# Reordered early loads and first chunks, a state update without products of zeros, and 64x64 tail products behind q, in an RWKV-7 and GCU kernel

## Chip, cores and metric

The kernel runs on one core of one Trainium2 chip. The metric is the device time of one execution in microseconds, from the runs of the program on that core; a comparison takes the medians of several runs of both kernels on the same chip. The profile is of one further execution.

## What is computed

Inputs r, k, v, w, a, b of shape (4, 8, 768, 40) (batch, heads, steps, head dimension) drive a recurrence with one 40x40 state per batch and head; its outputs, regrouped to 3072 tokens of 320 numbers, go through two matrix products with x * cos(x) between them.

```python
for t in range(768):
    y[:, :, t] = einsum('bhd,bhde->bhe', r_t, state)
    Sa = einsum('bhde,bhe->bhd', state, a_t)
    state = state * w_t[:, :, None, :] - einsum('bhd,bhe->bhde', Sa, b_t) + einsum('bhd,bhe->bhde', v_t, k_t)
x = y.transpose(0, 2, 1, 3).reshape(3072, 320)
h = x @ w_in                 # 320 x 2048
out = (h * cos(h)) @ w_out   # 2048 x 320
```

The two weight matrices come as 8-byte floats.

## The kernel before

**Chunks.** The 768 steps are cut into 24 chunks of C = 32. Within a chunk the recurrence is written as small matrix products, and the 32x32 triangular system that links its steps is solved for all 32 pairs of batch and head: VectorE (DVE) inverts it column by column (`inv_step`), or, for the first two groups of four chunks, in two halves of 16 (`pair_step` on DVE, then `pair_first` and `pair_second` as products on TensorE, PE). Inversion is done for four chunks at a time.

**Preparation of a pair of chunks** is `p1(c)`, four steps: `p1_w` transposes w (and for c < 4 scans it), `p1_a` transposes a and scales it (`a_W`), `p1_b` transposes the scaled b (`bn_b`), `p1_n` makes the products that the inversion starts from (`nps`, copied to `nt` and `noff`), and, before the change, also allocates and fills the tile `inv` on GpSimd (POOL).

**Preparation of one chunk** is `p2(c)`: `p2_v` transposes `vp` and `rp`, `p2_k` transposes `kn`, `p2_g` makes the Gram products (`gram`), from which DVE and ScalarE (ACT) make `ag` and part of `vvm`. `p2_in(c)` copies the landed v and r into `vp` and `rp` on POOL; `p2_kn(c)` makes `kn` and copies v into `vvm`, on POOL. When both have run for a chunk, `landed(c)` puts the loads of k, v and r of chunk c + 1 in the list of later work.

**The chunk itself** is `main(c)`, five steps: `ch_t` (t) transposes the state `qz`, `ch_q` (q) multiplies r with it, `ch_x` (x) and `ch_s` (s) solve, and `ch_z` (z) makes the new state and the outputs: on PE it first writes eight bf16 products of zeros over the whole of two PSUM tiles `dps` (64 rows x 288 columns each), so that all 128 rows, those between 40 and 64 of each half among them, hold defined numbers; then 32 fp32 products of `kn_b` with `vvm` and 32 of `bn_b` with `sm` add to them, each 40 columns of weights on 72 columns. DVE adds the result to `qz` and makes `yt`, POOL scales both. `tokens` (two steps later) writes `yt` to DRAM and, one step after that, reads it back as `xT`, the token-major operand.

**The second part** comes in pieces per pair of chunks g and per group j of 512 inner columns: `first_a` and `first_b` make `ph` = `xT` x `w_in` (two fp32 products of 128 rows per 128 columns, and one of the remaining 64 rows: the tails, `w_in_tail`), ACT and DVE make the cosine and the product `gT`, `second` makes `po`. In `first_b` the tails come ahead of the second half of the full products if the step just before was one of small tiles (`G["small"]`), and behind it otherwise. A tail is K = 64 rows on one half of the array: the two halves hold the two column groups e.

**PE tiles.** Operand positions set the tile: q works in 64x64 tiles (40x40 used), z in 32x64 tiles (32x40 used), the tails in 64x128, the full products in 128x128. Each fp32 product leaves two matmul records in the trace.

**Order.** Everything is one hand-written order (`tc.manual_schedule`), and each engine runs its part of it in that order. `step(work, of_inv, of_w, small)` issues one step, then the work in the list `waiting` that is due (`later(n, work)`: after n further steps), then `of_inv` steps of the inversion and `of_w` steps of the weight conversion. Conversion takes 20 blocks of 512 columns from 8-byte to 4-byte floats in four stages: `fetch` (DMA into `words`), `taken`, `mantissa`, `product` (DVE, ACT, POOL). Lines 964 to 1007 write out the beginning, up to z of chunk 0; `segs` (lines 1032 to 1075) gives, chunk by chunk, the order of the steps, with M as a place for a piece of the second part. `busy(n)` and `kept_busy(n)` put in bf16 matmuls of zeros as fillers.

**Loads.** `load(c, names)` issues four DMAs of 40 KB per name, by default on SyncE's queue (SP), which issues in order; those of a chunk's w, a, b go into buffers by the parity of c. `load(4, "ab")`, `load(5, "a")` and the fetches of the first two blocks of weights stand in the beginning before anything of chunk 1; loads of 6 and 7 come after the first preparation of 4 (`both_a`, lines 874 to 882).

Of the kernel before, what the change touches and what calls it, by code (L numbers as in the profile page):

```python
# [20 lines left out]
def kernel(  # L21
# [322 lines left out]
    def step(work, of_inv=0, of_w=0, small=False):  # L344


        before = list(waiting)
        work()
        G["small"] = small
        for w in before:  # L350
            w[0] -= 1
            if w[0] == 0:
                waiting.remove(w)
                w[1]()
        for steps, n in ((inv_steps, of_inv), (w_steps, of_w)):
            for _ in range(min(n, len(steps))):
                steps.pop(0)()
# [76 lines left out]
    def p1_n(c):  # L434
        ps = at("nps")
        for i in range(2):
            for j in range(4):
                for bb in range(B):
                    for e in range(2):
                        mm(  # L440
                            ps[blk[bb ^ e], e, (4 * i + j) * C : (4 * i + j + 1) * C],
                            G["bT", c + i][half[e], j, blk[bb]], G["aT", c + i][half[e], j, blk[bb]],
                            i == 0 and j == 0,
                        )

        if c % 4 == 0:
            G["nt"] = sb1.tile([P, C, 4, 2, HH], F32, tag="nt", name="nt")
            if c < 8:
                G["noff"] = sb2.tile([P, 4, 2, HH, C], F32, tag="rt", name="noff")
        for e in range(2):  # L450
            nc.scalar.copy(
                G["nt"][:, :, c % 4 : c % 4 + 2, e, :].rearrange("p t c j -> p c j t"),
                ps[:, e, : 2 * HH * C].rearrange("p (c j t) -> p c j t", c=2, j=HH),
            )
        if c < 8:
            for e in range(2):
                nc.scalar.copy(
                    G["noff"][:, c % 4 : c % 4 + 2, e, :, :].rearrange("p c j t -> p c (j t)"),
                    ps[:, e, : 2 * HH * C].rearrange("p (c n) -> p c n", c=2),
                )  # L460
        if c % 4 == 2:
            G["inv"] = sb1.tile([P, C * C], F32, tag="inv", name="inv")
            nc.gpsimd.memset(G["inv"], 0.0)
            nc.gpsimd.memset(G["inv"][:, :: C + 1], -1.0)


    def inv_start():

# [240 lines left out]
    def ch_z(c):  # L709
        ps = [at("dps") for _ in range(2)]  # L710
        sm = G["sm"]

        for bb in range(B):
            for e in range(2):
                mm(
                    ps[bb // 2][full[e], bb % 2, : 4 * N72], idle[blk[bb], :DP],
                    pick(idle[blk[bb]], 0, (0, 4), (1, N72)), True,
                )
        for s, n in ((0, kn_b[c % 2]), (1, bn_b[c % 7])):
            for j in range(4):  # L720
                o = C - C * (j // 2)
                for bb in range(B):
                    for e in range(2):
                        mm(
                            ps[bb // 2][half[e], bb % 2, j * N72 : (j + 1) * N72],
                            n[blk[bb], 2 * j + e, :D],
                            sm[e][blk[bb], j, :] if s else vvm[c % 2][blk[bb], 2 * j + e, o : o + N72],
                            False,
                        )
        wx, wc = G["wx", c], G["wc", c]  # L730
        yt = sb1.tile([P, 4, B, C], F32, tag="yt", name="yt")
        for bb in range(B):
            dp = ps[bb // 2][:, bb % 2]
            if c < NCH - 1:
                z = pick(qz[:, bb], C, (DP, 2), (NZ, 2), (1, D))
                nc.vector.tensor_tensor(z, pick(dp, 0, (2 * N72 + C, 2), (N72, 2), (1, D)), z, ALU.add)  # L736
                nc.gpsimd.tensor_tensor(  # L737
                    z, z,
                    wc.rearrange("p (f m b) -> p f m b", f=2, m=2)[:, :, :, bb]
                    .unsqueeze(3).to_broadcast([P, 2, 2, D]),  # L740
                    ALU.mult,
                )
            nc.vector.tensor_tensor(  # L743
                yt.rearrange("p (f m) b t -> p f m b t", f=2)[:, :, :, bb],
                pick(dp, D, (2 * N72 - D, 2), (N72, 2), (1, C)),
                pick(qz[:, bb], 0, (NZ - C, 2), (NZ, 2), (1, C)), ALU.add,
            )
        nc.gpsimd.tensor_tensor(  # L748
            yt.rearrange("p j b t -> p (j b) t"), yt.rearrange("p j b t -> p (j b) t"), wx, ALU.mult
        )  # L750
        later(2, lambda: tokens(c, yt))
# [36 lines left out]
    def first_b(g, j):  # L788
        xT, phs = G["xT", g], G["ph"]

        def tails(fresh):
            for f in range(2):
                for e in range(2):
                    mm(
                        phs[e][:, f, :], w_in_tail[full[e], j, f, :], xT[full[e], 2, :],
                        fresh and e == 1 and f == 0, False,
                    )


        if G["small"]:  # L800
# [65 lines left out]
    def p1(c):  # L866
# [7 lines left out]
        def both_a():  # L874
            p1_a(c)
            if c == 4:
                later(1, lambda: load(7, "w"))
                for i in range(2):
                    later(1, lambda i=i: load(6 + i, "ab"))
            elif c > 4 and c + 3 < NCH:  # L880
                for m in range(6):
                    later((9 if c == 6 else 2) + m, lambda m=m: load(c + 2 + m % 2, "wab"[m // 2]))
# [10 lines left out]
    def p2(c):  # L893
        def last():
            p2_g(c)
            if c + 1 < NCH:
                later(1, lambda: p2_in(c + 1))

        return [lambda: p2_v(c), lambda: p2_k(c), last]

# [8 lines left out]
    with tc.manual_schedule():  # L909
# [56 lines left out]
        first, other = p1(0), p1(2)  # L966
        for seg in first[:2]:
            step(seg)
        load(4, "ab")
        load(5, "a")  # L970
        for seg in (*other[:2], *first[2:], *other[2:]):
            step(seg)
        for m in range(2):
            w_work[m][0]()
        scanned(1)
        p2_in(0)
        p2_kn(0)
        inv_steps.extend(by_blocks(0))
        v, k, g = p2(0)
        v1, k1, g1 = p2(1)  # L980
        x0, s0, z0 = main(0)[2:]
        for n, seg, idle_n in ((6, v, 0), (0, k, 0), (0, g, 4), (4, x0, 6), (2, v1, 5)):
            for _ in range(n):
                inv_steps.pop(0)()
            step(seg)
            if seg is x0:
                w_work[2][0]()
                p2_kn(1)
# [6 lines left out]
        step(g1)  # L995
        busy(3)
        N_PAD = {0: 0, 19: 75}
        step(lambda: pair_first(0, 0, False))
        for m in range(3, 5):
            w_work[m][0]()  # L1000
        step(lambda: pair_second(0, 0, False), 0, 1)
        step(s0, 0, 3)
        busy(6)
        step(z0, 0, 4)
        busy(4)
        for n, c, name in ((3, 4, "w"), (5, 5, "w"), (7, 5, "b")):
            later(n, lambda c=c, name=name: load(c, name))
# [19 lines left out]
        for c in range(NCH):  # L1027
# [28 lines left out]
            elif c == 5:  # L1056
                pw, pa = p1(10)[:2]
                pb, pn = p8
                segs = [t, M, pb, q, M, pn, k, M, x, M, s, S6, M, pw, v, M, z, S7, M, g, M, pa, M]
            elif c % 4 == 0 and q0 < NCH:  # L1060
                pb, pn = p1(q0)[2:]
                segs = [t, v, M, q, M, k, x, M, g, M, s, pb, M, z, M, pn, M, M]
# [23 lines left out]
            for i, seg in enumerate(segs):  # L1086
# [6 lines left out]
                while seg is pn4 and w_steps:  # L1093
                    w_steps.pop(0)()
                if seg is not M:
                    step(seg, *((0, 0) if c < 3 and seg in (*firsts, *seconds) else fill), small=seg in (q, x, g, s, z, pn, pn4, *firsts, *seconds))
                    if seg not in (*firsts, *seconds) and (c < 2 or c == 2 and not done):
                        busy({s: 6, q: 5, v: 4, k: 4, z: 4}.get(seg, 3))
# [46 lines left out]
```

## Time and profile before

| What | Value |
|---|---|
| three runs | 811.71, 814.49, 815.9 us; median 814.49 |
| the profiled execution's own time | 814.53 us |
| its span, first to last instruction | 812.8 us |
| mean granted PE clock | 0.975 |
| PE, DVE, ACT, POOL busy | 758.7, 485.8, 387.1, 199.4 us |
| `po` products | 768 records, 223.3 us busy |
| `ph` full products, tails | 768 records, 186.7 us; 384 records, 54.7 us |
| products of zeros in z | 192 records, mean 311 ns, 8.3 us busy |
| `kn` and `bn` products in z | 1536 records each, 21.6 and 24.1 us busy |

A line of the timeline or of a group has the start in us (timeline only), the busy time, the engine, the line of the kernel, the operation, what it writes and reads, the shape, and xN for N records; in brackets stands the idle time of the engine just before and what ended it. Records of matmuls overlap, so a record's duration (200 to 500 ns) isn't its cost; the distance from one start to the next is. A line of a table by stretches has the stretch, its length, then the busy time and the instructions of PE, PEld (weight loads), DVE, ACT and POOL, the granted clock, the share of DMA time and GB/s. SPq is SP's queue of issues. All matmuls go through one helper and so carry line 101; they are told apart by tile names.

### The profile page before, as it was taken

The page shows a single profiled execution, that of the slowest core. Times are in us where ns is not written, and L with a number is a line of the kernel's source. Part 1 is how long each engine was busy: PE and PEld are TensorE (multiplying, and loading weights), DVE is VectorE, ACT ScalarE, POOL GpSimd, SP SyncE. Part 2 cuts the span into 40 slices and gives each one's busy share as a digit, 9 for nine tenths or more (in the row PEclk, how much of TensorE's full clock was granted, in tenths as well). Part 3 has the DMA queues.
Part 4 walks back from the last instruction along what each step waited for, and adds up shares of the span by engine and source line. Part 5 has one row for each costly group of instructions (what it writes and reads, how often), then busy time and mean ns, then how long its engine had stood idle before and what let it go on. Part 6 is the DMA issues. An engine that isn't in the chain of part 4 may idle for free.

```text
span 812.8 us, 39682 instructions
## 1 busy us (share of the span) xinstructions
PE 758.7 (93%) x17859; PEld 582.0 (72%) x17859; DVE 485.8 (60%) x1025; ACT 387.1 (48%) x723; POOL 199.4 (25%) x354
## 2 busy tenths in 40 slices
PE   3678799799999999999999999999999999999997
PEld 2545477677777777777777777777777777777775
DVE  6948858855743797553895554994346873332231
ACT  1326577454454346446436535534635445363352
POOL 5215634330404230230330330331130222201000
PEclk9878699999999999999999999999999999999999
DMA  8656553344244324324214314223220212101000
GB/s 123 120 142 170 158 141 99 54 114 67 51 94 92 67 42 72 69 89 70 59 36 74 78 47 71 55 45 68 45 45 21 45 37 57 23 14 36 19 17 16
DMA packets 183304, 55.79 MB, mean 69 GB/s; under 512 B 157152, under 2 KB 178656, under 8 KB 183136
## 3 DMA queue, kind: packets, MB, share of 16 engines
q1 hardware_dynamic: 180560, 51.95, 29.5%
q8 instruction: 140, 2.29, 1.2%
q10 hardware_dynamic: 2320, 0.98, 0.6%
q0 software_dynamic: 256, 0.33, 0.2%
q14 instruction: 28, 0.23, 0.1%
HBM read 42.07 MB, written 11.14 MB: 65 GB/s over the span
## 4 chain that ended last, share of the span: by engine, by line
PE 68%; DVE 15%; DMA 4%; issue 4%; ACT 4%; SPq 3%; POOL 1%; DVEq 0%; ACTq 0%; POOLq 0%
PE ph L101 23%; PE po L101 19%; PE x0ps L101 4%; PE dps L101 3%; DVE inv_tmp L478 3%; SPq L152 3%; PE gram L101 3%; DVE inv L482 3%; PE vT L328 2%; DVE rw L393 2%; PE sps L101 2%; PE busy L101 2%; PE nps L101 2%; PE qps L101 2%; PE sT L638 1%
## 5 line engine op out<-in xcount | busy, mean ns | idle before, releaser
L101 PE MATMUL po<-w_out_sb,gT 128*128 128x320 f32 x768 | 223.3, 439 | 0.0
L101 PE MATMUL ph<-xT,w_in_sb 128*128 128x256 f32 x768 | 186.7, 388 | 1.5 <-DMA xT<-xd 1.5
L101 PEld LDWEIGHTS po<-w_out_sb,gT 128*128 128x128 f32 x768 | 140.2, 190 | 54.2 <-issue 1.7
L101 PEld LDWEIGHTS ph<-xT,w_in_sb 128*128 128x128 f32 x768 | 140.5, 191 | 30.0 <-issue 10.6
L810 ACT ACTIVATE turns<-ph,rnd 128x512 f32<-128x512 f32 x96 | 64.1, 686 | 151.7 <-PE ph L101 151.3
L812 DVE SCALAR_TENSOR_TENSOR turns<-turns,ph 128x512 f32<-128x512 f32 x96 | 64.0, 684 | 116.0 <-ACT turns L810 115.8
L820 DVE TENSOR_TENSOR gT<-ph,turns 128x512 f32<-128x512 f32 x96 | 65.8, 686 | 37.8 <-ACT turns L817 37.8
L737 POOL TENSOR_TENSOR qz<-qz,wc 128x160 f32<-128x160 f32 x92 | 42.0, 475 | 158.5 <-DVE qz L736 157.9
L817 ACT ACTIVATE turns<-turns,half_pi 128x512 f32<-128x512 f32 x96 | 69.3, 722 | 3.1
L816 ACT ACTIVATE turns<-turns 128x512 f32<-128x512 f32 x96 | 60.1, 627 | 19.1 <-DVE turns L812 19.1
L101 PE MATMUL ph<-xT,w_in_tail 64*128 64x256 f32 x384 | 54.7, 402 | 0.0
L482 DVE TENSOR_TENSOR inv<-inv,inv_tmp 128x31 f32<-128x31 f32 (+15 forms) x124 | 51.2, 413 | 4.3
L570 POOL COPY vp<-nat_v 128x320 f32<-128x320 f32 x24 | 11.7, 489 | 164.4 <-DMA nat_v<-in_v_dram 121.1
L478 DVE TENSOR_TENSOR inv_tmp<-u,inv 128x31 f32<-128x31 f32 (+15 forms) x124 | 48.5, 391 | 2.3
L736 DVE TENSOR_TENSOR qz<-dps,qz 128x160 f32<-128x160 f32 x92 | 29.1, 316 | 33.3 <-PE dps L101 33.2
L393 DVE RECIPROCAL rw<-nat_w 128x320 f32<-128x320 f32 x20 | 42.8, 2142 | 0.0
L642 ACT COPY s<-sT 128x512 f32<-128x512 f32 x46 | 24.5, 585 | 37.8 <-PE sT L638 37.8
L101 PEld LDWEIGHTS ph<-xT,w_in_tail 64*128 64x128 f32 x384 | 33.3, 186 | 9.3 <-issue 5.6
L101 PEld LDWEIGHTS <-idle 32*64 32x64 bf16 (+2 forms) x443 | 21.5, 101 | 24.3 <-issue 19.7
L748 POOL TENSOR_TENSOR yt<-yt,wb 128x512 f32<-128x512 f32 x24 | 31.6, 1316 | 22.4 <-DVE yt L743 22.4
L702 DVE TENSOR_TENSOR sm<-sps,su 128x128 f32<-128x128 f32 x48 | 11.7, 285 | 34.1 <-ACT sm L697 31.3
L394 POOL TENSOR_TENSOR bn<-nat_b,rw 128x320 f32<-128x320 f32 x22 | 19.8, 900 | 48.5 <-DVE rw L393 38.5
(136 smaller groups left out, 1126.7 us busy)
## 6 DMA issues: line engine op xcount, KB each, us to landing
words<-in_moe_w_in_dram SPq DMA_DIRECT2D x8, 512.0 KB
nat_k<-in_k_dram SPq DMA_DIRECT2D x96, 40.0 KB
nat_v<-in_v_dram SPq DMA_DIRECT2D x96, 40.0 KB
nat_r<-in_r_dram SPq DMA_DIRECT2D x96, 40.0 KB
xd<-yt SPq DMA_DIRECT2D x48, 80.0 KB
out_dram<-ot SPq DMA_DIRECT2D x24, 160.0 KB
nat_b<-in_b_dram SPq DMA_DIRECT2D x88, 40.0 KB
nat_a<-in_a_dram SPq DMA_DIRECT2D x80, 40.0 KB
```

The lines of the kernel that those rows point to most:

```text
L101: nc.tensor.matmul(o, lhsT=lhsT, rhs=rhs, start=start, stop=stop, skip_group_check=True)
L393: nc.vector.reciprocal(rw, wn)
L478: nc.vector.tensor_tensor(tmp, u[:, j : j + 1, :j].to_broadcast([P, C - j, j]), x[:, j:, j : j + 1].to_broadcast([P, C - j, j]), ALU.mult,)
L482: nc.vector.tensor_tensor(x[:, j:, :j], x[:, j:, :j], tmp, ALU.subtract)
L736: nc.vector.tensor_tensor(z, pick(dp, 0, (2 * N72 + C, 2), (N72, 2), (1, D)), z, ALU.add)
L737: nc.gpsimd.tensor_tensor(z, z, wc.rearrange("p (f m b) -> p f m b", f=2, m=2)[:, :, :, bb] .unsqueeze(3).to_broadcast([P, 2, 2, D]), ALU. ...
L748: nc.gpsimd.tensor_tensor(yt.rearrange("p j b t -> p (j b) t"), yt.rearrange("p j b t -> p (j b) t"), wx, ALU.mult)
L810: nc.scalar.activation(n, u, ACTF.Identity, bias=rnd, scale=1.0)
L812: nc.vector.scalar_tensor_tensor(n, n, -ROUND, u, ALU.add, ALU.subtract)
L816: nc.scalar.activation(n, n, ACTF.Abs)
L817: nc.scalar.activation(n, n, ACTF.Sin, bias=half_pi, scale=-2.0 * math.pi)
L820: nc.vector.tensor_tensor(gT[:, 2 * e : 2 * e + 2].rearrange("p f t -> p (f t)"), us[e], ns[e], ALU.mult)
```

## The change

Six edits:

1. In z the eight products of zeros go. The `kn` products take all 64 columns of the padded tile (columns 40 to 63 hold zeros) and write all 64 rows; the first of them for each half has the start flag. The `bn` products stay at 40.
2. `G["small"]` now holds the kind of the last small step. Where it was q, the tails are cut into two halves of their output rows: eight 64x64 products instead of four of 64x128. Elsewhere they stay as they were.
3. The fill of `inv` leaves `p1_n` for the first group: `inv_space()` is called in the beginning after `p2_kn(0)`.
4. In the beginning, `b` of chunk 4 and the fetches of weight blocks 0 and 1 move behind the first step of p2(0); x of chunk 0 gets six inversion steps ahead of it instead of four; the weight steps behind the pair steps, s and z of chunk 0 become 2, 2, 4, 2 (they were 0, 1, 3, 4); `p2_in(2)` comes four steps after p2(1) instead of one.
5. Loads of chunks 6 and 7: a, a, b, b instead of a, b, a, b.
6. Chunk 5: the order of its second half changes, z ahead of the w transpose (pw) and v.

```diff
-        G["small"] = small
+        G["small"] = small and G["kind"]
...
-        if c % 4 == 2:
-            G["inv"] = sb1.tile([P, C * C], F32, tag="inv", name="inv")
-            nc.gpsimd.memset(G["inv"], 0.0)
-            nc.gpsimd.memset(G["inv"][:, :: C + 1], -1.0)
-
+        if c % 4 == 2 and c > 2:
+            inv_space()
+
+    def inv_space():
+        G["inv"] = sb1.tile([P, C * C], F32, tag="inv", name="inv")
+        nc.gpsimd.memset(G["inv"], 0.0)
+        nc.gpsimd.memset(G["inv"][:, :: C + 1], -1.0)
...
-        for bb in range(B):
-            for e in range(2):
-                mm(
-                    ps[bb // 2][full[e], bb % 2, : 4 * N72], idle[blk[bb], :DP],
-                    pick(idle[blk[bb]], 0, (0, 4), (1, N72)), True,
-                )
...
-                            ps[bb // 2][half[e], bb % 2, j * N72 : (j + 1) * N72],
-                            n[blk[bb], 2 * j + e, :D],
+                            ps[bb // 2][(half if s else full)[e], bb % 2, j * N72 : (j + 1) * N72],
+                            n[blk[bb], 2 * j + e, : D if s else DP],
                             sm[e][blk[bb], j, :] if s else vvm[c % 2][blk[bb], 2 * j + e, o : o + N72],
-                            False,
+                            not s and j == 0,
...
-                    mm(
-                        phs[e][:, f, :], w_in_tail[full[e], j, f, :], xT[full[e], 2, :],
-                        fresh and e == 1 and f == 0, False,
-                    )
+                    for to in (full if G["small"] == "q" else [every]):
+                        mm(
+                            phs[e][to, f, :], w_in_tail[full[e], j, f, to], xT[full[e], 2, :],
+                            fresh and e == 1 and f == 0, False,
+                        )
...
-                for i in range(2):
-                    later(1, lambda i=i: load(6 + i, "ab"))
+                for n in "ab":
+                    for i in range(2):
+                        later(1, lambda n=n, i=i: load(6 + i, n))
...
-                later(1, lambda: p2_in(c + 1))
+                later(4 if c == 1 else 1, lambda: p2_in(c + 1))
...
-        load(4, "ab")
+        load(4, "a")
         load(5, "a")
         for seg in (*other[:2], *first[2:], *other[2:]):
             step(seg)
-        for m in range(2):
-            w_work[m][0]()
         scanned(1)
         p2_in(0)
         p2_kn(0)
+        inv_space()
...
-        for n, seg, idle_n in ((6, v, 0), (0, k, 0), (0, g, 4), (4, x0, 6), (2, v1, 5)):
+        for n, seg, idle_n in ((6, v, 0), (0, k, 0), (0, g, 4), (6, x0, 6), (2, v1, 5)):
             for _ in range(n):
                 inv_steps.pop(0)()
             step(seg)
+            if seg is v:
+                for m in range(2):
+                    w_work[m][0]()
+                load(4, "b")
...
-        step(lambda: pair_first(0, 0, False))
+        step(lambda: pair_first(0, 0, False), 0, 2)
...
-        step(lambda: pair_second(0, 0, False), 0, 1)
-        step(s0, 0, 3)
+        step(lambda: pair_second(0, 0, False), 0, 2)
+        step(s0, 0, 4)
         busy(6)
-        step(z0, 0, 4)
+        step(z0, 0, 2)
...
-                segs = [t, M, pb, q, M, pn, k, M, x, M, s, S6, M, pw, v, M, z, S7, M, g, M, pa, M]
+                segs = [t, M, pb, q, M, pn, k, M, x, M, s, S6, M, z, M, S7, M, pw, v, M, g, pa, M]
...
                 if seg is not M:
+                    G["kind"] = "q" if seg is q else "other"
```

## Prediction

> **What bounds the kernel now.** I read the page first: its PE row, its forty slices and its chain; then the table by stage; then the timeline of each stage that the change touches. The page says that TensorE (PE) is busy 93% of the span, but the table of stretches says where that means something.
>
> ```profile
> PE 758.7 (93%) x17859; PEld 582.0 (72%) x17859; DVE 485.8 (60%) x1025; ACT 387.1 (48%) x723; POOL 199.4 (25%) x354
> ...
> 26.00:49.00 23.00, 15.75 (x490) 10.30 (x491) 19.75 (x47) 7.91 (x18) 6.17 (x11) 0.83 0.61 137
> 49.00:66.00 17.00, 13.15 (x474) 8.07 (x473) 4.66 (x14) 4.87 (x10) 2.06 (x3) 0.70 0.60 150
> ...
> 110.00:165.00 55.00, 49.54 (x1182) 39.51 (x1182) 42.23 (x73) 32.42 (x58) 20.61 (x30) 0.97 0.38 93
> 165.00:812.00 647.00, 632.41 (x14715) 490.64 (x14703) 361.82 (x796) 307.61 (x576) 130.98 (x237) 1.00 0.26 54
> ```
>
> From 165 us on PE is busy 632 of 647 us at full clock: there a PE microsecond saved is a microsecond of the run, and so is a stall removed. Before 165 the granted clock (0.70 to 0.97) and the many `busy` fillers say the opposite: PE waits on chains of loads, VectorE (DVE) steps and ACT copies, and what counts is the wait that ends last.
>
> Four places matter. First, chunk 1's first transposes:
>
> ```profile
> 44.87 0.66 PE L328 MATMUL vT<-ident,vp 128*128 128x128 f32 x4 [0.48 <-POOL vp L570]
> 47.13 0.66 PE L328 MATMUL vT<-ident,rp 128*128 128x128 f32 x4 [1.60 <-POOL rp L570]
> ...
> 29.37 1.89 SPq L152 DMA_DIRECT2D nat_b<-in_b_dram  x4
> 31.36 2.55 SPq L152 DMA_DIRECT2D nat_a<-in_a_dram  x4
> 33.95 0.92 SPq L235 DMA_DIRECT2D words<-in_moe_w_in_dram  x2
> 34.98 2.33 SPq L152 DMA_DIRECT2D nat_k<-in_k_dram  x4
> 37.41 4.66 SPq L152 DMA_DIRECT2D nat_v<-in_v_dram  x4
> 42.12 2.81 SPq L152 DMA_DIRECT2D nat_r<-in_r_dram  x4
> ```
>
> PE waits for a POOL copy, that waits for `r` of chunk 1, and `r` is issued last on SP, behind `b` of chunk 4 and two 512 KB weight fetches whose landing stalls the queue. Second and third, single waits in chunks 3 and 5; fourth, what the state update and the tail products cost in the full stage (chunk 13):
>
> ```profile
> 160.02 0.72 PE L328 MATMUL aps<-ident,nat_a 128*128 128x128 f32 x4 [1.57 <-DMA nat_a<-in_a_dram]
> ...
> 242.87 0.72 PE L101 MATMUL below<-rt,half 32*32 32x16 f32 x64 [1.44 <-DVE yt L743]
> ...
> 252.73 0.48 PE L101 MATMUL ph<-xT,w_in_sb 128*128 128x256 f32 x1 [1.48 <-DMA xT<-xd]
> ...
> 431.38 0.81 PE L101 MATMUL qps<-rT,s 40*40 40x32 f32 x64
> 432.13 1.14 PE L101 MATMUL ph<-xT,w_in_tail 64*128 64x256 f32 x8
> 433.19 1.99 PE L101 MATMUL ph<-xT,w_in_sb 128*128 128x256 f32 x8
> ...
> 447.36 0.33 PE L101 MATMUL dps<-idle 32*64 32x288 bf16 x8
> 447.51 0.86 PE L101 MATMUL dps<-vvm,kn 32*40 32x72 f32 x62
> ```
>
> Durations of overlapping matmuls say little; I use start to start. Chunk 13: q takes 431.38 to 432.13 (0.75), the tails 1.06, the zeros 0.15; the whole state update is 0.15 + 1.48 (447.36 to 448.99).
>
> **What the Trainium skill says.** "TensorEngine Tiling (Array Packing)", Key Properties: changing the tiling mode, not just the tile, drains the engine. The trace agrees: eight `ph` records take 1.73 us between others of their mode and 1.92 between two mode changes, so a change costs about 0.1 on either side. "TensorE: Matmul & The Clock Gate", LDWEIGHTS: the load's time goes by the columns, not the rows. The trace agrees as far as it goes: median load 107 to 111 ns at 40 columns, about 187 at 128. "Runtime: NRT & Kernel Launch", Instruction fetch mechanics: instructions come by the engine's own DMA in blocks of 256. The page's instruction queues (2.29 MB) fit, and so does a PE stop of 2.65 us between two `x0ps` records (37.97 to 40.62) while the weight fetches fill the DMA engines.
>
> **The change part by part.**
>
> *State update (24 times).* It drops eight bf16 products of zeros; the first products of `kn` write 64 columns with the start flag instead. In the steady stage this removes 0.15 us of starts; but PE then issues about one weight load and one matmul per 8.3 ns (gram: 62 records in 0.53), so if issue is the limit only 16 x 4.2 ns = 0.07 is gone. The wider loads add 24 columns. From 32 columns (`x0ps`, 12.7 ns a record) to 40 (`dps`, 13.0) costs 0.3 ns, so 24 more would cost 0.9 ns x 64 = 0.06 at worst. Bounds per chunk: +0.06 to -0.15; I take -0.10. For the 21 chunks after 165 us: **-2.1** (+1.3 to -3.2). The first three lie under waits: 0.
>
> *Tails.* Counting the built order, 16 of 48 tail groups stand right behind q and become eight 64x64 products instead of four 64x128. q is already in 64x64 tiles (40x40 rounded up), so one of three mode changes goes. Now: q's last record starts at 432.00, the tails at 432.13, their second round 0.32 later and then every 0.216: 0.12 of drain and 0.10 of exposed first load. The products themselves should cost the same: four rounds of 0.216, two tiles a round now, four then. q shows four tiles starting 6 ns apart, and the state update eight at once in rounds of 0.062, which is near streaming rate. 16 x 0.2 = **-3.2** (-1.6 to -3.7).
>
> *Chunk 5.* z goes two places earlier, with a product piece between it and the pair step S7. Now S7 waits 1.66 start to start (241.20 to 242.87) for DVE to free PSUM, and `ph` waits 1.75 (250.98 to 252.73) for xT. A piece is 2 to 3 us, which covers the first; z and its stores come some 4.6 us sooner (wT 0.87, vT 0.88, ph 1.82, tail 1.06), which covers the second. New: gram, `aps` and sT stand together; sT wants gram's buffer, which DVE frees late, as at 180.94 to 181.67: +0.8. Net **-2.6** (-0.5 to -3.4).
>
> *Loads for chunks 6 and 7.* `a` of 7 now goes ahead of `b` of 6: four DMAs, 1.97 us on SP. `aps` waits 1.84 for it (158.18 to 160.02), **-1.8**. The eight `ph` behind it run at half clock (0.43 against 0.216 each, 1.7 in all), because PE idled: bounds 0 to -3.5. `b` of 6 moves behind; its user stands at 172.7 and has 10 us of cover.
>
> *First chunks.* SP loses 1.89 (`b`) and 0.92 plus landing waits (words) ahead of `k`, `v`, `r` of chunk 1: 12 issues at 0.49 after 31.4 end at 37.3, so `r` lands near 39.3 instead of 46.5. The wait of 1.87 on `rp` goes. The `inv` fill (0.96 + 0.15 on POOL) moves behind the copies; DVE needs it at 34.3, POOL would be done at 31.5: nothing. x0 gets two more inverse steps ahead of it, which fills DVE's wait of 1.50 at 40.7. What is late next: PE's own fillers at half clock, then the fetch stops at 37.97 (2.65) and 53.66 (1.46). The words still have to come and now land at 38 to 42, beside x0, so I credit little of these. Weight steps come earlier (2, 2, 4, 2 behind the first steps instead of 0, 1, 3, 4): DVE, idle 12 of 17 us from 49 to 66, takes up to one block (0.42 + 0.42 + 0.68 + 0.69 = 2.2) off its later list. Against that POOL now runs two sign products (1.15 each) ahead of qz, where one was, and p2_in of chunk 2 stands behind yt (1.72): the transposes of c = 1 may wait for it 0.4, +1.2 and +0.4. Sum: -1.9 - (0 to 2.65) - (0 to 2.2) + (0 to 1.6); I take **-3.5** (0 to -6.7). That it reaches 165 us rests on the chain: PE without gaps from 99.8 to 116.7, DVE weight steps from there to 149.6, then the loads; all of it starts from the first chunks.
>
> Sum: 2.1 + 3.2 + 2.6 + 1.8 + 3.5 = 13.2. The profiled execution took 814.5 us (span 812.8), as the median did (814.5): **801.3**.
>
> **The rivals.**
> 1. *The head start is swallowed.* Fillers, fetch stops and the POOL queue give the 3.5 and half of the 1.8 back before 165: 805.7. For it: DVE and PE both had slack there, so neither was bound by those loads alone. Against it: the chain runs through them.
> 2. *Small tiles don't pay.* Issue, not streaming, is the limit: state update +1.3 instead of -2.1, tails -1.6: 801.3 + 3.4 + 1.6 = 806.3. For it: the steady 8.3 ns.
> 3. *More comes.* Half clock at 160 and one fetch stop vanish: 801.3 - 1.7 - 2.6 = 797.
> 4. *Slower:* the four quarter tiles run one after another. Sixteen rounds of 0.216 = 3.46 instead of 0.86 make q and tails 0.62 + 3.46 + 0.1 = 4.18 against 1.81: +37.9 in 16 places against 10.0 from the rest: 842. It decides above 0.62 + 0.1 + n x 0.216 = 1.81 + 10.0/16, that is from 8 rounds on. Against it: q's own four tiles overlap.
> 5. *The early order does harm:* words land later, beside x0 and the fetch, and the first third loses 5 instead of gaining 5.3: 811.6.
>
> **How the numbers follow.** Forecast 0.45, rivals in order 0.18, 0.12, 0.14, 0.04, 0.07. A run of this kernel tells 0.5% (4.1 us) from no change. Faster by more: forecast and rivals 1 to 3 but for their tails, 0.86; within: 0.09; slower: 0.05. The range, 794.5 to 808, holds forecast, 1, 2 and 3 and leaves out the other two.
>
> **What would show it.** Right: `dps` 1.45 to 1.6 us a chunk with no zeros; q plus tails 1.55 to 1.65; `rp` of chunk 1 copied near 40; no wait over 1 at `aps` of chunk 7, S7 or xT of chunk 6; `ph` of chunk 2 (109.9) 3 to 4 us sooner. Wrong: tail groups of over 2 us behind q, a kn half over 0.8, or a first `ph` no earlier.

## The result and the profile after

The changed kernel takes 814.82 us (median of 20 runs, 806.02 to 819.82) against 813.90 for the kernel before (20 runs, 808.84 to 817.30): ratio 0.9993, 95% interval 0.9973 to 1.0013. Nothing was gained; 801.3 was forecast and 794.5 to 808 was the range.

The profiled execution of the changed kernel took 818.75 us (span 817.0), one of the slower of its runs: its trace shows where time goes, and somewhat more of it than a median run loses. The page's PE row, and the stretches that answer those of before:

```profile
PE 757.7 (93%) x17795; PEld 580.6 (71%) x17795; DVE 486.1 (60%) x1025; ACT 387.0 (47%) x723; POOL 200.9 (25%) x354
```

```profile
26.00:49.00 23.00, 18.54 (x672) 13.00 (x670) 21.25 (x48) 9.21 (x20) 7.40 (x13) 0.85 0.61 135
49.00:66.00 17.00, 9.35 (x311) 5.45 (x299) 7.20 (x22) 6.09 (x12) 3.24 (x5) 0.73 0.73 208
110.00:165.00 55.00, 51.99 (x1201) 42.10 (x1200) 42.18 (x74) 34.50 (x63) 21.17 (x30) 0.97 0.40 94
165.00:817.00 652.00, 631.95 (x14631) 487.93 (x14629) 361.59 (x796) 305.69 (x571) 130.35 (x236) 0.99 0.26 54
```

From 26 to 49 us PE does more than before (672 products instead of 490): the head start is there. From 49 to 66 it does less (311 instead of 474). After 165 us it holds 84 products less than before but needs 5 us more (652 instead of 647), with 20 us idle instead of 15.

The places where the forecast expected something, in the timeline of PE after the change (the rows near 433 and 448 us belong to chunk 12, as do the rows that the prediction labels chunk 13):

```profile
41.63 0.60 PE L328 MATMUL vT<-ident,vp 128*128 128x128 f32 x4
43.63 0.66 PE L328 MATMUL vT<-ident,rp 128*128 128x128 f32 x4 [1.40 <-POOL rp L572]
...
48.66 0.49 PE L101 MATMUL below<-bn,noff 32*32 32x16 f32 x37
52.63 0.42 PE L101 MATMUL below<-bn,noff 32*32 32x16 f32 x27 [3.48 <-issue]
...
158.01 1.04 PE L328 MATMUL aps<-ident,nat_a 128*128 128x128 f32 x8
158.89 1.89 PE L101 MATMUL ph<-xT,w_in_sb 128*128 128x256 f32 x8
...
432.81 0.81 PE L101 MATMUL qps<-rT,s 40*40 40x32 f32 x64
433.45 1.14 PE L101 MATMUL ph<-xT,w_in_tail 64*64 64x256 f32 x16
434.52 1.99 PE L101 MATMUL ph<-xT,w_in_sb 128*128 128x256 f32 x8
...
448.00 0.87 PE L101 MATMUL dps<-vvm,kn 32*64 32x72 f32 x60
...
449.52 1.14 PE L101 MATMUL ph<-xT,w_in_tail 64*128 64x256 f32 x8
```

`rp` of chunk 1 is transposed 3.5 us sooner; `aps` of chunk 7 waits for nothing and the `ph` behind it run at full clock; the tails behind q start 0.64 after q and last 1.07; the state update lasts 1.52 with no zeros. The sign of all this is what was forecast, though `rp` comes later than "near 40" and q with its tails takes 1.71 in this place. What was not forecast are the stops with `<-issue`, that is, with no engine or DMA that PE waited for:

```profile
210.38 0.71 PE L101 MATMUL gram<-rT,vT 40*32 40x32 f32 x61
213.26 0.21 PE L101 MATMUL gram<-rT,vT 40*32 40x32 f32 x1 [2.17 <-issue]
213.60 1.72 PE L328 MATMUL aps<-ident,nat_a 128*128 128x128 f32 x8
...
218.60 2.92 PE L101 MATMUL ph<-xT,w_in_sb 128*128 128x256 f32 x8
...
566.06 0.41 PE L101 MATMUL dps<-sm,bn 32*40 32x72 f32 x20
567.34 0.67 PE L101 MATMUL dps<-sm,bn 32*40 32x72 f32 x37 [0.87 <-issue]
...
649.77 0.28 PE L101 MATMUL gram<-rT,vT 40*32 40x32 f32 x12 [1.33 <-issue]
649.98 0.88 PE L101 MATMUL sps<-x,rt 32*32 32x72 f32 x64
650.79 4.08 PE L101 MATMUL po<-w_out_sb,gT 128*128 128x320 f32 x8
```

They stand in the middle of rows of small products that nobody holds up. Before the change the same rows ran through:

```profile
212.66 0.73 PE L101 MATMUL gram<-rT,vT 40*32 40x32 f32 x62
...
565.16 1.07 PE L101 MATMUL dps<-sm,bn 32*40 32x72 f32 x62
...
646.64 0.73 PE L101 MATMUL gram<-rT,vT 40*32 40x32 f32 x62
647.29 0.88 PE L101 MATMUL sps<-x,rt 32*32 32x72 f32 x64
648.11 2.42 PE L101 MATMUL po<-w_out_sb,gT 128*128 128x320 f32 x8
```

Behind two of the stops TensorE runs slower for a while: `ph` takes 2.92 instead of 1.89 (granted clock 0.50 to 0.63 from 213.6 to 221.4 us) and `po` 4.08 instead of 2.42 (0.66 from 650 to 655).

Now number PE's instructions in the order of time: loads, products, and also PE's semaphore and drain instructions (307 before, 330 after), which the timeline leaves out and which take places too. Call an instruction's number within a run of 256 its place. Every such stop stands at one and the same place, the 194th: a new block begins there. This holds in the traces of all 18 kernels here: behind 165 us, every gap of over 0.7 us from start to start that is put down to issue, with no semaphore instruction in it, stands there. PE's instructions come in packets of 16 KB; the page shows 140 of them (both kernels alike), one per 256 of 36,025 instructions before and 35,920 after:

```profile
q8 instruction: 140, 2.29, 1.2%
```

In both traces PE goes on 1.3 to 1.6 us after such a packet has landed, at each of these stops. Summed over the stops above 0.5 us at that place (start to start): before, 13.8 us ahead of 165 us and 2.0 (3 stops) behind it; after, 12.8 and 8.5 (7 stops, of 115 block ends there). To the 6.5 us more come about 3.4 of lower clock (`aps` and `ph` at 213 to 221, `po` at 651).

### The profile page after: what moved, and what is told of

It reads as the page before. It is cut to its first block, busy times and chain, and to the rows that moved or that the text cites. A ratio compares the mean times of both kernels' runs of the same rounds, so it can differ in the third digit from the quotient of the medians.

```text
span 817.0 us, 39570 instructions
## 1 busy us (share of the span) xinstructions
PE 757.7 (93%) x17795; PEld 580.6 (71%) x17795; DVE 486.1 (60%) x1025; ACT 387.0 (47%) x723; POOL 200.9 (25%) x354
## 4 chain that ended last, share of the span: by engine, by line
PE 69%; DVE 10%; DMA 6%; SPq 4%; issue 4%; ACT 4%; POOL 2%; DVEq 0%; ACTq 0%; POOLq 0%
PE ph L101 23%; PE po L101 20%; PE x0ps L101 4%; SPq L152 3%; PE dps L101 3%; PE gram L101 3%; PE vT L328 3%; DVE rw L393 2%; PE sps L101 2%; PE qps L101 2%; DVE inv_tmp L480 2%; PE nps L101 2%; DVE inv L484 2%; PE sT L640 1%; DMA xd<-yt 1%
## 5 line engine op out<-in xcount | busy, mean ns | idle before, releaser
L101 PE MATMUL ph<-xT,w_in_tail 64*128 64x256 f32 (+1 forms) x512 | 54.0, 393 | 0.0
L101 PEld LDWEIGHTS ph<-xT,w_in_tail 64*128 64x128 f32 (+1 forms) x512 | 31.7, 160 | 9.0 <-issue 5.3
L628 ACT COPY vvm<-gram 128x256 f32<-128x256 f32 x24 | 8.8, 368 | 46.0 <-DVE ag L623 45.6
```

The lines of the kernel that those rows point to most:

```text
L101: nc.tensor.matmul(o, lhsT=lhsT, rhs=rhs, start=start, stop=stop, skip_group_check=True)
```

## The experiments

*Theory A:* the edits pay, but their instruction counts move all later block ends; an end that falls into dense small products leaves PE waiting for the next block. The new state update drops 16 instructions per chunk (8 products, 8 loads), the 64x64 tails add 16 in chunks 4 to 19: by loads and products, everything from chunk 4 to 19 stands 64 places earlier in its block, then up to 128. *Theory B:* the edits do not pay. *Theory C:* the early order is swallowed by its own weight fetches; the rest pays.

The recorded texts count loads and products alone. The numbering of the traces, semaphore instructions included, differs a little: with the new tails about one more of those comes per chunk, so q of chunk 4 stands 60 places earlier than before, and q of chunk 19 only 45. Where a text says "the same place", read "within some 20".

**Places restored, and moved without the change.** In the first kernel the zeros stay in chunks 0 to 3 and 20 to 23, so that the counts of loads and products are those of before (the traces differ by 1 place in chunk 4 and 16 in chunk 19); the second is the kernel before, without the zeros in chunks 0 to 3 (PE waits for others there).

```diff
+        short = 4 <= c < 20
+        if not short:
+            for bb in range(B):
+                for e in range(2):
+                    mm(
+                        ps[bb // 2][full[e], bb % 2, : 4 * N72], idle[blk[bb], :DP],
+                        pick(idle[blk[bb]], 0, (0, 4), (1, N72)), True,
+                    )
```

(and the old products where `short` is false); the second kernel has `short = c < 4`, and all else of the kernel before.

First: 

> The changed kernel with the products of zeros kept in chunks 0 to 3 and 20 to 23, so that every TensorE instruction of chunks 4 to 23 stands at the same place within its block of 256 as in the kernel before. Theory A (the edits pay, and what they save is spent again at the ends of instruction blocks, because the shorter stream has moved those ends by 64 records): the stops without a releaser after 165 us fall from 11.2 us back to about 2.3, and the time is 807 (804 to 810). Theory B (the edits themselves do not pay): 814 to 815, as the changed kernel. Theory C (the early order is swallowed by its own weight fetches whatever the alignment, the rest pays): 810 to 812.

Second: 

> The kernel before, with one edit: the products of zeros left out in chunks 0 to 3, where TensorE waits for others anyway. It issues 64 records fewer, all before chunk 4, and from there on is the old stream moved by 64 records against the block ends. Theory A: slower, 818 to 823 against 814, with stops without a releaser at the same steps as in the changed kernel (inside gram of chunk 5, in sps of chunk 5, near 566 and 648 us). Theories B and C: no difference, 813 to 815.

Measured: first 810.35 against 813.34, ratio 0.9948 (0.9928 to 0.9968). That is just outside the 804 to 810 of A and inside the 810 to 812 of C. Second **825.50**, ratio 1.0136 (1.0088 to 1.0184): 32 products fewer with their loads, where PE waits anyway, and 12 us slower, more than A had (818 to 823). Its stops over 0.5 us behind 165 sum to some 9.8 us, and three of them stand in or beside the rows where the changed kernel has its own:

```profile
211.66 0.73 PE L101 MATMUL gram<-rT,vT 40*32 40x32 f32 x62
214.77 1.17 PE L328 MATMUL aps<-ident,nat_a 128*128 128x128 f32 x8 [2.38 <-issue]
...
572.50 0.58 PE L101 MATMUL dps<-sm,bn 32*40 32x72 f32 x29
573.95 0.48 PE L101 MATMUL dps<-sm,bn 32*40 32x72 f32 x30 [0.86 <-issue]
...
655.84 0.32 PE L101 MATMUL sps<-x,rt 32*32 32x72 f32 x4
657.27 0.85 PE L101 MATMUL sps<-x,rt 32*32 32x72 f32 x60 [1.11 <-issue]
```

Neither B nor C can explain this. The first kernel gained only 3 to 4 us, since one stop of 2.33 us came in chunk 5 and one of 1.43 at 662.6.

**Parts alone.** Arithmetic alone (`4 <= c < 20` as above, so the counts of loads and products hold) and order alone (state update and tails as before):

> The kernel before with the two edits of the arithmetic alone, the new state update only in chunks 4 to 19: the 16 records that it saves in a chunk are the 16 that the tail groups add, so the block ends stay where they were. Theory A: 16 x (0.08 + 0.06 to 0.2) = 2 to 4.5 us faster, 809.5 to 812, state update 1.53 a chunk. Theory B: 813 to 815.

> The changed kernel with the old state update and the old tail products: the order of loads, first chunks and chunk 5 alone, no TensorE instruction more or fewer than before. Theory A: 808.5 to 811.5, since the waits at aps of chunk 7, at S7 and at xT of chunk 6 go and no new block stops come after 165 us. Theories B and C: 813 to 815; C shows the stops of 3.7, 2.7 and 3.0 us before 85 us as in the changed kernel and no gain left at 165 us.

Measured 815.70, ratio 1.0021 (0.9994 to 1.0048), and 813.38, ratio 0.9981 (0.9951 to 1.0012). Both missed. In the trace the arithmetic does what it should: from chunk 8 to chunk 20 it gains 2.6 us on the kernel before (0.2 a chunk), but it had come 2.5 late to chunk 8, and a stop of 1.15 at 669 follows. The order alone is 4.6 us ahead at q of chunk 4, then stops of 1.46 and 1.83 us stand in chunk 5 (231.2 and 234.9), and 0.5 is left at chunk 7; one of 1.59 at 645.8 took the rest. That stop fell into a stretch with the very instructions of before, which in the profile of before has none: a single execution places its stops only roughly.

**A large move.** The kernel before with 44 more one-column products ahead of chunk 4.

```diff
-        N_PAD = {0: 0, 19: 75}
+        N_PAD = {0: 0, 4: 44, 19: 75}
...
-            if c == 19:
+            if c in N_PAD and c:
                 shifted(N_PAD[c])
```

> The kernel before with 44 one-column products more ahead of chunk 4 (the kernel has 75 such products ahead of chunk 19, which take 1.9 us), which move all later instructions by 88 places against the block ends. Theory A, with a least time of 3.6 us from block end to block end laid over the instruction times of the kernel before (its own places give 1.1 us of stops after 165 us, a move of 64 records the other way 9.0): stops of about 50 us, so 855 to 870. Theory B, that the edits' arithmetic and order cost what they cost wherever the block ends lie: 1.1 us more than before, 814 to 816.

Measured 828.66 (two runs), ratio 1.0171 (1.0133 to 1.0210). The sign is A's, the size is not: 14 us instead of 40 to 55. In this trace blocks whose own instructions took 1.2 to 1.8 us end in no stop over 0.3 us where the block ahead lasted 6.0 us or more, and in stops of 0.6 to 2.1 where it lasted 4.5 or less. So a block's instructions may be there ahead of time, and "3.6 us for each block" is no law.

**Dense runs by themselves.** 512 products of 32 x 64 by one column, added ahead of chunks 2 and 12 of the kernel before; they write a scratch tile that nothing reads.

```diff
+        def dense(n):
+            ps = [at("dps") for _ in range(2)]
+            for m in range(n):
+                bb, e = m % 4, m // 4 % 2
+                mm(ps[bb // 2][full[e], bb % 2, :1], idle[blk[bb], :DP], idle[blk[bb], :1], True)
...
+            if c in (2, 12):
+                dense(512)
```

> The kernel before with 512 extra one-column products in tiles of 32 rows by 64 columns ahead of chunk 2 and as many ahead of chunk 12: each is four whole blocks, so all other instructions keep their places. Theory A: ahead of chunk 12 a block takes about 3.5 us whatever is in it, so 14 us for four; ahead of chunk 2, where the DMA engines are busier, more, 16 to 22 us. If instructions come as fast as TensorE issues them (8.3 ns for a load and its product, as in gram): 4.3 us each.

Measured in the timeline, ahead of chunk 12 and of chunk 2:

```profile
446.38 1.23 PE L101 MATMUL dps<-idle 32*64 32x1 bf16 x128 [2.39 <-issue]
450.13 1.23 PE L101 MATMUL dps<-idle 32*64 32x1 bf16 x128 [2.51 <-issue]
...
102.95 1.57 PE L101 MATMUL dps<-idle 32*64 32x1 bf16 x128 [2.52 <-issue]
106.95 1.23 PE L101 MATMUL dps<-idle 32*64 32x1 bf16 x128 [2.43 <-issue]
110.68 1.23 PE L101 MATMUL dps<-idle 32*64 32x1 bf16 x128 [2.50 <-issue]
```

Every row holds 128 products, with their loads a whole block. From start to start a block takes 3.66 to 4.02 us, of which PE is stopped 2.6 to 3.0; the 256 instructions themselves take some 1.05 (4.1 ns each; the granted clock was 0.51 and 0.55 in these stretches). In the trace the packet starts 1.0 to 1.5 us after the block begins, takes 0.9 to 1.4, and PE goes on 1.2 to 1.5 after it has landed. The other traffic, 1.58 MB in 4393 packets at chunk 2 and 0.97 MB in 5992 at chunk 12, makes no difference that shows: 3.73 to 4.00 ahead of chunk 2, 3.66 to 4.02 ahead of chunk 12. "16 to 22" for chunk 2 was wrong, 3.7 for a block is right for dense blocks one after another. The whole took 844.15 us in one run.

The Trainium skill, "Runtime: NRT & Kernel Launch", Instruction fetch mechanics, says that the next 16 KiB block is fetched while the current one runs and that crossing a boundary is mostly hidden. Most crossings agree: behind 165 us, 112 of 115 block ends before the change and 108 of 115 after show no stop over 0.5 us. Dense small products don't: there 2.6 to 3.0 of 3.7 us are exposed. No length of a block makes it safe in these traces; stops of 0.5 to 1.5 us in the profile after also follow blocks whose own instructions took 3.7 to 4.2 us.

**Other places for the changed kernel.** Zeros kept in chunks 0, 1 and 20 to 23 (32 places earlier than before by loads and products; 29 in chunk 4 and 14 in chunk 19 by the trace); the same move with all edits kept and 16 one-column products added ahead of chunk 1; and the kernel before moved by the same 32.

```diff
+        short = 2 <= c < 20
```
```diff
-        N_PAD = {0: 0, 19: 75}
+        N_PAD = {0: 0, 1: 16, 19: 75}
```
```diff
+        short = c < 2
```

> The changed kernel with the zeros kept in chunks 0, 1 and 20 to 23 only: all from chunk 4 on stands 32 places earlier in its block than where the zeros are kept in chunks 0 to 3. Theory A, the least block time of 3.6 us laid over the instruction times of that kernel: stops after 165 us of 0.9 us instead of 6.4, so 804 to 807 against 810.35. Theory B: 810 to 811.

> The changed kernel, all its edits kept, with 16 one-column products added ahead of chunk 1, where TensorE waits anyway: from chunk 4 on everything stands 32 places earlier in its block than in the kernel before, as in the kernel with zeros in chunks 0 and 1 that took 808.2, instead of 64. Theory A: 807 to 810, faster than the changed kernel (814.8) although it only has 32 instructions more; the stops of over 1 us near 210, 234, 566 and 648 us are gone. Theory B: 814.8 or slightly more.

> The kernel before without the products of zeros in chunks 0 and 1 only, so with the same places from chunk 4 on as the kernel that took 808.2, but the old order and the old arithmetic. If places alone had made that kernel fast, this one takes 807 to 809. If the edits pay 5 us at equal places: 812 to 814.5, as the kernel before has few stops after 165 us (2.3 us) to lose.

Measured: 808.22, ratio 0.9921 (0.9893 to 0.9949); **805.88, ratio 0.9902 (0.9874 to 0.9929)**; and 820.68, ratio 1.0100 (1.0068 to 1.0132). With 16 products that compute nothing the changed kernel becomes 1% faster than before. A had 804 to 807 for the first and 807 to 810 for the second; both lie 1 us outside. The first kernel's trace (the fastest of its nine runs) has no stop over 0.5 us behind 165, and its span is 801.3; the second has three, 2.4 us in sum, of which 1.06 stays in the `gram` that had 1.52 near 648. Where the changed kernel stopped for 2.17 inside `gram` of chunk 5, the second shows:

```profile
204.95 0.71 PE L101 MATMUL gram<-rT,vT 40*32 40x32 f32 x61
205.73 1.06 PE L328 MATMUL aps<-ident,nat_a 128*128 128x128 f32 x8
...
554.73 0.87 PE L101 MATMUL dps<-sm,bn 32*40 32x72 f32 x62
555.53 1.13 PE L101 MATMUL ph<-xT,w_in_tail 64*128 64x256 f32 x8
```

No idle time, and `aps` 1.06 instead of 1.72. The third kernel was to lie at 812 to 814.5; it is 7 us slower than before, with stops of 2.00, 1.40, 1.35 and 1.28. Its places are not quite those of the first two: 2 to 3 earlier in chunk 4, 17 to 18 in chunk 19. So a place that is good for one order of instructions needn't be good for another; that the order alone decides isn't shown.

**Chunk 5, the loads, the first chunks.** The held kernel (810.35) with chunk 5 in the old order; the kernel before with the loads of 6 and 7 alone; and with the first chunks alone (the change's parts at `inv_space`, `last`, `load(4, ...)`, and lines 964 to 1007).

```diff
-                segs = [t, M, pb, q, M, pn, k, M, x, M, s, S6, M, z, M, S7, M, pw, v, M, g, pa, M]
+                segs = [t, M, pb, q, M, pn, k, M, x, M, s, S6, M, pw, v, M, z, S7, M, g, M, pa, M]
```
```diff
-                for i in range(2):
-                    later(1, lambda i=i: load(6 + i, "ab"))
+                for n in "ab":
+                    for i in range(2):
+                        later(1, lambda n=n, i=i: load(6 + i, n))
```

> The changed kernel with the zeros kept in chunks 0 to 3 and 20 to 23, and with chunk 5 in the order of before. If the early z in chunk 5 packs two dense steps (sps and the state update) into one block, so that the stop of 2.3 us at 232.6 replaces the two waits it removed: 807 to 809.5 against 810.35 with the new order. If the chunk 5 order is worth the 2.6 that was forecast: 812.5 to 813.

> The kernel before with the order of the loads for chunks 6 and 7 alone; no TensorE instruction is added or moved. Forecast -1.8, so 811.5 to 812.5 against 813.5; in the trace 1.8 to 3.3 us less between sps of chunk 3 and q of chunk 4, the upper end if the eight ph behind aps run at 0.216 instead of 0.43. If it is swallowed: 813.5 with the wait at aps of chunk 7 still over 1 us.

> The kernel before with the early loads and first chunks of the changed kernel alone. Forecast -3.5, so 810; the starts of chunk 1 come 4 to 5 us sooner and block stops of 2 to 3.5 us in below, dps and gram take part of it back. If the rest of the head start is swallowed ahead of 165 us: 813 to 814.

Measured: 810.53, ratio 0.9933 (0.9904 to 0.9962), beside 0.9948 (0.9928 to 0.9968) with the new order: no difference, and neither of the two figures that were expected; 813.07, ratio 1.0003 (0.9982 to 1.0023); 813.57, ratio 0.9984 (0.9958 to 1.0010). None of the three shows a gain.

- Chunk 5: with the old order S7 waits 1.74 for `yt`, and `bT` waits 1.68 for POOL's `bn`; with the new order the first is gone, of the second 0.57 of idle time is left (1.41 with the old), and a stop of 2.33 inside the tails stands there.
- Loads alone: `aps` of chunk 7 waits for no DMA and `ph` takes 1.89, not 3.53. PE is 2.4 us ahead at q of chunk 4, 0.9 at chunk 7, 0.4 at chunk 21; the stops are 1.74 at 174.1 and 1.34 at 644.8.
- First chunks alone: 4.9 us ahead at q of chunk 4, 1.2 behind at chunk 7: a stop of 1.73 at 191.6, the wait at S7 (1.66), which it does not change, and a new wait of 1.68 for `bn`. The time lies where it was expected if the gain is lost ahead of 165 us (813 to 814), but the trace says that it is lost behind. The other traces agree: q of chunk 4 starts at 181.7 to 185.2 us in the six with the old first chunks (the dense runs left out) and at 176.9 to 182.1 in the seven with the new ones and at most 16 products more (six of these with the new loads too). So C is wrong at that point. Ahead of it much is lost, though: 4.6 us in the mean at gram of chunk 1 are 1.1 at the first `ph` of chunk 2 (107.6 to 109.9 against 103.9 to 110.8).

**Place or delay?** To tell a place from a mere delay ahead of chunk 1: 144, 80, 32 and 24 one-column products there instead of 16, all else as in the changed kernel.

```diff
-        N_PAD = {0: 0, 19: 75}
+        N_PAD = {0: 0, 1: 144, 19: 75}
```

> The changed kernel with 144 one-column products ahead of chunk 1, 128 more than in the kernel that took 805.9: one whole block more, so every later instruction has the same place in its block. Theory A: 806 to 809.5, up to 3.7 for one block more to fetch, less what lies under TensorE's waits in chunk 1, and again no stop of over 1.5 us after 165. If the gain came from a small delay ahead of chunk 1, 128 products more destroy it: 814 or more.

> The changed kernel with 80 one-column products ahead of chunk 1: half a block away from the place of 16 and 144. Theory A: stops of over 5 us in sum after 165 us, 813 to 824. If the gain came from a delay or from the clock: between the times with 16 and with 144.

> The changed kernel with 32 one-column products ahead of chunk 1: the places of the kernel before in chunks 4 to 19, as with the zeros kept in chunks 0 to 3, which took 810.35. Theory A: 809 to 812. By a delay or the clock: 805 to 807, as with 16.

> The changed kernel with 24 one-column products ahead of chunk 1, between the places of 16 (805.9) and 32 (theory A: 809 to 812). Theory A: 805 to 810, and a stop sum after 165 us of 1 to 5 us that the time follows. By a delay or the clock: 805 to 807.

| Products ahead of chunk 1 | us | ratio to before | stops over 0.5 us behind 165 us | the profiled execution, us |
|---|---|---|---|---|
| 0 (the changed kernel) | 814.82 | 0.9993 (0.9973 to 1.0013) | 8.5 | 818.75 |
| 16 | 805.88 | 0.9902 (0.9874 to 0.9929) | 2.4 | 803.94 |
| 24 | 807.46 | 0.9904 (0.9870 to 0.9937) | 5.3 | 811.05 |
| 32 | 810.89 | 0.9950 (0.9927 to 0.9973) | 5.2 | 808.36 |
| 80 | 824.73 | 1.0106 (1.0051 to 1.0162) | 14.5 | 823.51 |
| 144 = 16 + 128 | 809.14 | 0.9938 (0.9912 to 0.9964) | 3.2 | 809.36 |

Three times lie where A had them, and 80 lies 0.7 us above its range. Two signs of A failed: one stop of 1.79 stands at 173.7 us with 144, where none over 1.5 was to come, and the stops with 24 sum to 5.3, not 1 to 5. 80 products make the kernel 19 us slower than 16; 64 more bring back 15.6 of that, since with 144 each instruction has its place again (q of every chunk stands at exactly the same place of 256 in both traces). The 3.3 us that 144 costs over 16 fit the one dense block more (3.7). The loss from a mere delay, or from the clock, would not be undone by 64 products more. The stop sums are of one execution and follow the medians only roughly: 24 and 32 have the same sum and differ by 3.4 us, and the profile with 24 is of its slowest run. The longest stop with 80 was this, and the same row with 144 has none:

```profile
647.32 0.65 PE L101 MATMUL sps<-x,rt 32*32 32x72 f32 x36
649.90 0.47 PE L101 MATMUL sps<-x,rt 32*32 32x72 f32 x28 [1.94 <-issue]
```

```profile
642.39 0.88 PE L101 MATMUL sps<-x,rt 32*32 32x72 f32 x64
```

## Why the prediction was wrong

*State update: right.* 1.60 to 1.53 a chunk where nothing else interferes; -0.10 was forecast. The 0.07 is what the prediction gave for the case that issue is the limit. A load of 64 columns takes 131 ns (median) and one of 40 took 111, but that costs nothing that shows. (The prediction's "107 to 111 ns at 40 columns" mixes in 32 columns: there it is 104 to 106, at 40 columns 111 to 120.)

*Tails: right in kind, a third high.* q with its tails took 1.81 before in each of the 16 places. It takes 1.64 in ten of them and 1.71 to 1.82 in six: -0.17 in the median, but -0.13 in the mean, 2.1 us in all where 3.2 was counted. q's share fell from 0.75 to 0.63 and the tails' from 1.06 to 1.00, which fits a mode change that is gone and a first load that is better covered, though no run here tells the two apart ("TensorEngine Tiling (Array Packing)", Key Properties: a change of mode drains the engine). The two edits together gave 2.7 us in the 11 chunks from 8 to 19 of the kernel that took 808.22 (8.7 us ahead of before at chunk 8, 11.4 at chunk 19): 0.245 a chunk, where 0.30 was counted and the two figures above give 0.20.

*Loads for chunk 7: right, and low.* The wait and the half clock behind it both went (1.57 and 1.64 us of the profile before; both are gone in the trace of the loads alone), where only 1.8 was taken.

*First chunks: half right.* `r` lands earlier, but SP is done with its issues only at 39.9 (37.3 was counted), `rp` is copied at 43.1, not near 40 (46.6 before), and a wait of 1.40 for it stays. Gram of chunk 1 is 4.8 us sooner. In the profile after this is lost again: the first `ph` of chunk 2 starts at 110.8, not 3 to 4 us before 109.9. In between, block stops sum to 12.0 us against 9.9 before, with 3.66 in `below`, 2.70 in dps and 3.00 in gram of chunk 2 (start to start); waits of 2.34 for `sm` and 2.08 for `yt` come in, where before had one of 1.69 for `w_in_tail`. The stops were named as what is late next, but they were taken to cost no more than before.

*Chunk 5: wrong.* Both waits went, 1.66 and 1.75. The forecast said of what comes instead only that sT wants gram's buffer (it waits 0.45). In the profile after, stops of 0.95 and 0.20 us and a wait of 0.87 for `bn` came as well, and chunk 5 gained nothing (35.4 us from q to q, 35.2 before). In the kernel that took 808.22 it takes 33.8, with one step of the arithmetic in it: half of the 2.6 at most, and that is one execution. The wait for xT isn't gone for good either: it is 0.92 with 16 products and 1.86 with 144.

*The step that failed* is the sentence on which the sum stands: "there a PE microsecond saved is a microsecond of the run, and so is a stall removed." After 165 us PE is not bound by its work alone. In dense stretches it is bound by the arrival of its instructions, which depends on where each block of 256 ends, and the edits moved all these places. The prediction had seen stops at blocks, in the prelude only, and never counted how many instructions the edits take out and put in ahead of each later step. That term was not mis-sized; it was missing. It was worth as much as all the rest: 814.82 with the places that the change happened to get, 805.88 with 16 products more. And the kernel before shows the knob: `shifted(N_PAD[c])` puts 75 one-column products that nothing reads ahead of chunk 19 (1.9 us, from 632.4 to 634.3). The prediction passed them over; whether 75 was chosen for the counts of before, no run here shows. None of the rivals named it; rival 5 (811.6) came nearest in time, by another mechanism.

*What of the 13.2 is there:* at the best of six places the changed kernel is 8 us faster than before (ratio 0.9902), and the fastest run of the kernel with 808.22 took 802.98 us. Runs at about the same place (within 27 of 256 in chunks 4 to 19) make a fairer pair:

| Place of q of chunk 4 | old order and arithmetic, us | new, us |
|---|---|---|
| 189 to 193 | 813.90 (before) | 810.35 (zeros in 0 to 3 and 20 to 23), 810.89 (32 products) |
| 158 to 161 | 820.68 (no zeros in 0 and 1) | 808.22 (zeros in 0, 1 and 20 to 23), 805.88 (16) |
| 128 to 129 | 825.50 (no zeros in 0 to 3) | 814.82 (the changed kernel) |
| 21 to 33 | 828.66 (44 products) | 824.73 (80) |

The new is faster in each row, by 3 to 15 us (the kernel before itself gave medians of 813.3 to 815.2 beside these runs): the edits pay, against B, but what they pay depends on the place, and the kernel before stands at the best of its four. The sum was thus some 5 us high at the best places: 0.05 to 0.1 a chunk and half of chunk 5 account for 2 to 3 of it, the first chunks for the rest as far as the runs tell.

*Open:* why a packet at times starts only 2 to 3 us after the block ahead began (2.98 ahead of the stop of 1.40 at 447.7 in the kernel before moved by 32), while in dense runs it takes 1.0 to 1.5. So neither a stop's size nor a good place could be foretold, as the misses of the kernels with 44 products and with the kernel before moved by 32 show.

## What to carry to other kernels

Before you add up savings on a TensorE that is "93% busy", look at the stops that the trace puts down to issue, number PE's instructions, semaphore instructions too, and see whether they stand at one place modulo 256; if so, each edit that adds or removes instructions also moves every later block end, and a fair comparison holds that count or tries a few. A few one-column products where PE waits anyway are a cheap knob: here 16 of them were worth 9 us, and 80 cost 10. Where two dense steps of small products meet, a piece of long products between them may give the next block time to come; no run here tried that by itself.

## What had not been expected of the hardware

- TensorE fed with small products takes 3.66 to 4.02 us for 256 instructions although it issues them in some 1.05 (4.1 ns each).
- Removing 32 products with their loads made a kernel 12 us slower (825.50), removing 16 made it 7 slower (820.68), and adding 16 to another made that 9 us faster.
- Some stops cost more than themselves: behind an idle time of 1.33 us `po` ran 4.08 us instead of 2.42, behind one of 2.17 `ph` 2.92 instead of 1.89, at a granted clock of 0.50 to 0.66. Length alone doesn't decide it: behind 1.96 us of idle time at 232.6 in the kernel that took 810.35, the granted clock was 1.00.
